# Loading the first keys uncast on SyncE's queue, in a fused pooled-attention and mixture-of-experts kernel

## The chip, the cores and the metric

The kernel runs on one core of one Trainium2 chip. The metric is the device time of one execution in microseconds (us); the kernel before was quoted at 178.73 us, the median of 6 runs (178.28 to 179.21).

Five engines work on such a core: TensorE (PE in the profile, PEld for its weight loads), VectorE (DVE), ScalarE (ACT), GpSimd (POOL) and SyncE (SP). Data is moved by 16 DMA engines. GpSimd feeds them through the *software queue*, which in this kernel casts float32 to bfloat16 on the way (a row of 18,432 B read is written as 9,216 B); what SyncE and ScalarE send through their queues here is not cast.

## The reference, cut to what matters

```python
# q, k, v: (8 batches, 8 heads, 576, 64) float32
k_p = k.reshape(B, H, 72, 8, D).mean(axis=3)          # keys pooled by 8
v_p = v.reshape(B, H, 72, 8, D).mean(axis=3)
attn = softmax(q @ k_p.T / sqrt(D)) @ v_p
x = attn, rearranged to (4608, 512)
logits = x @ phi                                       # phi: (512, 32)
slot_input = softmax(logits, axis=0).T @ x             # 32 slots, 4 for each of 8 experts
slot_out[e] = relu(slot_input[e] @ w1[e]) @ w2[e]      # w1: 512x1024, w2: 1024x512, float32
out = softmax(logits, axis=1) @ slot_out               # (4608, 512) float32
```

The inputs are 62 MB of float32 and the output is 9.4 MB. The kernel computes in bfloat16.

## The kernel before: the parts that matter here

The batches are worked on in four pairs. For each pair, k, q and v are loaded whole (one tile is 128 partitions by 72 rows of 64 values), cast by the software queue. All these tiles share four buffers, so a load waits until PE has finished with the tile four loads earlier. The weights w1 and w2 follow in the same queue.

```python
big = ctx.enter_context(tc.tile_pool(name="big", bufs=4))

def load_pair(src, pair, name):
    t = big.tile([128, NT, D], BF, name=name, tag="big")
    nc.gpsimd.dma_start(out=t, in_=src[2 * pair:2 * pair + 2].rearrange("b h (i t) d -> (b h i) t d", t=NT))
    return t

w1_sb = persist.tile([128, E, DJ, F], BF)
...
phi_f = persist.tile([128, DM // 128, NS], FP)
nc.sync.dma_start(out=phi_f, in_=moe_phi.rearrange("(p j) e -> p j e", j=DM // 128))   # 64 KB
k_sb[0] = load_pair(k, 0, "k_sb")
q_sb[0] = load_pair(q, 0, "q_sb")
... # identity matrix, made by GpSimd
v_sb[0] = load_pair(v, 0, "v_sb")
...
for pair in range(1, NP):          # k, q, v of the other pairs, then w1, then w2
    ...
```

PE pools k (`pool_ps`), transposes q (`q_ps`), pools v, and so on; `place_phi` spreads phi into a constant on VectorE (`spread`) for a later matmul.

The softmax here doesn't subtract the row's maximum and nothing guards it: scores larger than these inputs give would overflow.

Of the kernel before, what the change touches and what calls it, by code (L numbers as in the profile page):

```python
# [8 lines left out]
FP = mybir.dt.float32  # L9
BF = mybir.dt.bfloat16  # L10
# [8 lines left out]
def kernel(  # L19
# [10 lines left out]
    nc = tc.nc  # L30

    B, H, S, D = q.shape
# [3 lines left out]
    E = moe_w1.shape[0]  # L36
# [8 lines left out]
    NT = S // NI  # L45
# [13 lines left out]
    big = ctx.enter_context(tc.tile_pool(name="big", bufs=4))  # L59
# [7 lines left out]
# [6 lines that stand above are left out]
# [23 lines left out]

    k_sb, q_sb, v_sb = [None] * NP, [None] * NP, [None] * NP

    phi_f = persist.tile([128, DM // 128, NS], FP)
    nc.sync.dma_start(out=phi_f, in_=moe_phi.rearrange("(p j) e -> p j e", j=DM // 128))  # L100

    hT = persist.tile([128, E, FJ, NS], BF)
    k_sb[0] = load_pair(k, 0, "k_sb")
    q_sb[0] = load_pair(q, 0, "q_sb")
    ident = consts.tile([128, 128], BF)
    make_identity(nc, ident)
# [31 lines left out]
    for r in range(2):  # L138
        rows = slice(r * D, (r + 1) * D)
        nc.vector.tensor_copy(out=iphi[rows, :, 0:D],  # L140
                              in_=ident[rows, rows].rearrange("p d -> p () d").to_broadcast([D, H, D]))
# [7 lines left out]
    so = persist.tile([128, DM], BF)  # L149
    recC = persist.tile([128, 1], FP)  # L150
    recR = persist.tile([128, NSMALL + (NO - NSMALL) // 2, 4], FP)

    for pair in range(1, NP):
        for dst, src, name in ((k_sb, k, "k_sb"), (q_sb, q, "q_sb"), (v_sb, v, "v_sb")):
# [244 lines left out]
    for n in range(E // NG):  # L399
        for half in range(F // 512):  # L400
            cols = slice(half * 512, (half + 1) * 512)
            h_ps = ps_m.tile([128, 512], FP, name="h_ps", tag="m")
            for j in range(DJ):
                for g in range(NG):
                    e = n * NG + g
# [112 lines left out]
```

## Time and profile before

| what | before |
|---|---|
| span of the profiled run | 175.8 us (175.764) |
| DMA engines, 2.5 to 140 us | share 0.97 to 1.08 in windows of 2.5 us, about 214 GB/s written |
| effective start of the weight-and-input stream, mean engine | 3.72 us |
| last weights landed, mean engine / slowest engine | 148.78 / 149.58 us |
| first and last output packet | 149.52 / 173.62 us |

First the profile's 40 equal slices of the span for the kernel before: a digit is the busy share of the slice in tenths, and the last row is what the DMA engines moved. Below them are its queue totals: packets, megabytes written, and packet time as a share of 16 engines.

```profile
PE   7992899699999999999999898799975295787000
...
DMA  4999999999999999999999999999999999999994
GB/s 72 206 222 210 222 214 210 224 212 220 210 223 212 218 216 210 223 211 216 214 214 216 214 214 218 214 214 218 213 218 214 208 193 167 334 362 425 420 418 190
...
q0 software_dynamic: 6816, 30.94, 86.8%
q1 hardware_dynamic: 3872, 9.50, 13.9%
```

The DMA engines are full from the second slice to the last but one. The software queue writes bfloat16 at about 214 GB/s, which means that it reads float32 at about 428 GB/s; the output at the end is plain float32 at about 420 GB/s. So this is a kernel bound by its DMA engines: its time is when they start, plus their work, plus any holes.

Next the same kernel in windows of time. The columns are: window and its length, busy time (and count) of PE, PEld, DVE, ACT and POOL, PE's granted clock, the share of the DMA engines, and GB/s. A window's share may exceed 1 because a packet is counted where it begins.

```profile
0.00:2.00 2.00, 0.81 (x2) 0.28 (x3) 1.10 (x11) 1.26 (x1) 0.95 (x6) 1.00 0.08 24
2.00:3.00 1.00, 1.00 (x4) 0.43 (x3) 0.20 (x1) 0.23 (x2) 0.93 (x3) 1.00 1.34 147
3.00:4.00 1.00, 1.00 (x4) 0.33 (x3) 0.88 (x5) 0.00 (x0) 1.00 (x3) 1.00 0.04 9
4.00:5.00 1.00, 1.00 (x3) 0.30 (x2) 1.00 (x7) 0.00 (x0) 0.11 (x1) 1.00 1.14 230
...
20.00:40.00 20.00, 17.39 (x188) 12.04 (x186) 8.02 (x22) 13.28 (x26) 1.59 (x3) 0.84 1.03 215
```

Until 2.6 us only the 64 KB of phi have been moved. The large packets counted from 2 to 3 us are the first fourteen of the software queue; they are slow and occupy their engines until about 4 us, and from then on the engines run at full rate. That poor stretch is what the change is after; I call it empty below.

The trace also has one record per DMA packet, with queue, start, duration and size. Each load ends on each of the 16 engines with a 4-byte completion packet. In this text *landing on the mean engine* is the mean of those 16 times and *on the slowest engine* the last of them. The sizes that matter in the records of the kernel before:

| packet | median duration |
|---|---|
| software queue, one row of k, q or v (9,216 B written, 18,432 B read) | 0.700 us (one begins every 0.684 us) |
| software queue, one row of w1 (8,192 B written) | 0.625 us |
| SyncE's queue, 8,192 B of output | 0.314 us |
| software queue, 512 B piece of the last w2 | 0.060 us |

### The profile page before, as it was taken

The numbers are of one execution on the slowest core, as the hardware profiler recorded it, in microseconds if no ns is written. First come the engines' busy times: TensorE is split into PE (matmuls) and PEld (weight loads), VectorE is DVE, ScalarE is ACT, GpSimd is POOL, SyncE is SP. The second block draws the span as 40 slices with busy tenths as digits, with TensorE's granted clock in tenths as the row PEclk, the third lists the DMA queues.
The fourth block names the chain that finished last, engine by engine and source line by source line (L and its number), as shares of the span: only waits on it lengthen the run. The fifth ranks groups of instructions, "written<-read, shape, count | busy, mean of one in ns | idle before, by whom it ended". The sixth has DMA issues, their size and how long they took to land.

```text
span 175.8 us, 3531 instructions
## 1 busy us (share of the span) xinstructions
PE 140.2 (80%) x1469; PEld 88.2 (50%) x1469; DVE 90.9 (52%) x252; ACT 80.3 (46%) x146; POOL 19.7 (11%) x39
## 2 busy tenths in 40 slices
PE   7992899699999999999999898799975295787000
PEld 2452677464987667876676435563564132321000
DVE  5401612456387796877978718953351005799000
ACT  3021289456395696946979724011110003699000
POOL 6001110002011071111113002101400000000000
PEclk9999699855599999999999758559999569999655
DMA  4999999999999999999999999999999999999994
GB/s 72 206 222 210 222 214 210 224 212 220 210 223 212 218 216 210 223 211 216 214 214 216 214 214 218 214 214 218 213 218 214 208 193 167 334 362 425 420 418 190
DMA packets 10702, 40.64 MB, mean 231 GB/s; under 512 B 832, under 2 KB 6336, under 8 KB 6592
## 3 DMA queue, kind: packets, MB, share of 16 engines
q0 software_dynamic: 6816, 30.94, 86.8%
q1 hardware_dynamic: 3872, 9.50, 13.9%
q8 instruction: 11, 0.18, 0.4%
q14 instruction: 3, 0.02, 0.0%
HBM read 61.93 MB, written 9.44 MB: 406 GB/s over the span
## 4 chain that ended last, share of the span: by engine, by line
PE 45%; DMA 30%; ACT 10%; DVE 3%; issue 2%; POOL 1%; POOLq 0%; ACTq 0%
DMA w_xs<-in_moe_w_dram 14%; DMA q_sb<-in_q_dram 11%; PE pool_ps L181 8%; PE sc L250 8%; PE u_ps L262 8%; PE G_ps L279 6%; DMA k_sb<-in_k_dram 5%; PE q_ps L195 5%; PE f_ps L464 3%; ACT w_sb L466 2%; DVE xs L268 2%; PE lg_ps L273 2%; PE fold_ps L206 2%; ACT ex_1634 L251 1%; ACT ex_1635 L251 1%
## 5 line engine op out<-in xcount | busy, mean ns | idle before, releaser
L268 DVE TENSOR_TENSOR xs<-u_ps,rec 128x384 bf16<-128x384 f32 x72 | 39.4, 551 | 1.6
L250 PE MATMUL sc<-qT,kp 64*72 64x288 bf16 x128 | 24.4, 327 | 0.8 <-ACT ex_1635 L251 0.4
L267 DVE RECIPROCAL rec<-u_ps 128x4 f32<-128x4 f32 x72 | 12.4, 175 | 20.2 <-PE u_ps L262 19.9
L195 PE MATMUL q_ps<-ident,q_sb 128*128 128x128 bf16 x144 | 13.7, 250 | 5.3 <-DMA q_sb<-in_q_dram 5.0
L201 DVE COPY qT<-q_ps 128x768 bf16<-128x768 bf16 x16 | 8.8, 551 | 16.7 <-PE q_ps L195 16.6
L195 PEld LDWEIGHTS <-q_sb 128*128 128x128 bf16 x144 | 10.4, 113 | 7.3 <-DMA q_sb<-in_q_dram 5.3
L464 PE MATMUL f_ps<-so,cT 128*128 128x512 bf16 (+1 forms) x46 | 11.0, 331 | 3.6 <-DVE so L453 1.2
L250 PEld LDWEIGHTS <-kp 64*72 64x72 bf16 x128 | 8.9, 111 | 8.8 <-issue 3.5
L279 PE MATMUL G_ps<-xs,ee 128*128 128x512 bf16 x36 | 11.8, 471 | 0.4 <-ACT ee L274 0.4
L181 PE MATMUL pool_ps<-pmat,v_sb 128*128 128x128 bf16 x144 | 11.2, 240 | 0.0
L199 ACT COPY qT<-q_ps 128x768 bf16<-128x768 bf16 x8 | 6.4, 799 | 9.8 <-PE q_ps L195 9.7
L114 PEld LDWEIGHTS <-zeros 128*128 128x128 bf16 x51 | 5.7, 120 | 9.6 <-issue 5.9
L184 ACT CAST kpar<-pool_ps 128x512 bf16<-128x512 f32 (+1 forms) x12 | 5.5, 485 | 10.7 <-PE pool_ps L181 10.6
L181 PEld LDWEIGHTS <-v_sb 128*128 128x128 bf16 x144 | 9.7, 109 | 0.8 <-issue 0.3
L181 PE MATMUL pool_ps<-pmat,k_sb 128*128 128x128 bf16 x144 | 9.7, 219 | 0.2
L466 ACT ACTIVATE o_sb_2313<-f_ps,recR 128x256 f32<-128x256 f32 x1 | 0.5, 474 | 19.7 <-PE f_ps L464 19.7
L464 PEld LDWEIGHTS <-cT 128*128 128x128 bf16 x46 | 4.3, 96 | 10.0 <-issue 7.6
L181 PEld LDWEIGHTS <-k_sb 128*128 128x128 bf16 x144 | 8.4, 98 | 1.2 <-DMA k_sb<-in_k_dram 0.6
L468 DVE TENSOR_SCALAR w_sb<-f_ps,recR 128x512 f32<-128x512 f32 x12 | 8.3, 746 | 0.0
L184 ACT CAST vpar<-pool_ps 128x512 bf16<-128x512 f32 (+1 forms) x12 | 5.6, 480 | 5.8 <-PE pool_ps L181 5.7
L453 DVE TENSOR_SCALAR so<-so_ps_2183,recC 128x256 bf16<-128x256 f32 x1 | 0.5, 484 | 14.5 <-PE so_ps_2183 L449 14.5
L466 ACT ACTIVATE w_sb<-f_ps,recR 128x512 f32<-128x512 f32 x12 | 7.7, 684 | 0.6
(165 smaller groups left out, 240.2 us busy)
## 6 DMA issues: line engine op xcount, KB each, us to landing
w_sb<-in_moe_w_dram POOLq DMA_DIRECT2D x7, 1024.0 KB, 28.3
out_dram<-w_sb SPq DMA_DIRECT2D x6, 1024.0 KB, 8.5
k_sb<-in_k_dram POOLq DMA_DIRECT2D x4, 1152.0 KB, 17.8
q_sb<-in_q_dram POOLq DMA_DIRECT2D x4, 1152.0 KB, 17.9
v_sb<-in_v_dram POOLq DMA_DIRECT2D x4, 1152.0 KB, 16.2
w_big<-in_moe_w_dram POOLq DMA_DIRECT2D x4, 1024.0 KB, 30.4
w_qT<-in_moe_w_dram POOLq DMA_DIRECT2D x2, 1024.0 KB, 34.8
w_xs<-in_moe_w_dram POOLq DMA_DIRECT2D x2, 512.0 KB, 24.2
```

The source lines that it names most:

```text
L181: nc.tensor.matmul(out=ps[:, r].rearrange("p n i -> p (n i)"), lhsT=src[:, tt:tt + 2, :].rearrange("p t d -> p (t d)"), rhs=pmat, start=(t ...
L184: nc.scalar.copy(out=dst[:, r0:r0 + nr], in_=ps[:, 0:nr])
L195: nc.tensor.transpose(out=ps[:, t].rearrange("p n i -> p (n i)"), in_=q_sb[pair][:, tt:tt + 2, :].rearrange("p t d -> p (t d)"), identity= ...
L201: nc.vector.tensor_copy(out=dst, in_=ps)
L250: nc.tensor.matmul(out=ps[:, r, 0:S // 2], lhsT=kp[pair][rows, n], rhs=qT[pair][rows, n], start=True, stop=True)
L262: nc.tensor.matmul(out=ps[rows, hh], lhsT=ex[b][:, hh].rearrange("p r t -> p (r t)")[:, c:c + rows.stop - rows.start], rhs=vp[(2 * pair + ...
L267: nc.vector.reciprocal(out=rec, in_=ps[:, :, XW])
L268: nc.vector.tensor_tensor(out=xs[pair][:, t, qd * HQ:(qd + 1) * HQ, :], in0=ps[:, :, 0:XW], in1=rec.rearrange("p h -> p h ()").to_broadcas ...
L279: nc.tensor.matmul(out=ps, lhsT=ee[:, t].rearrange("p g s -> p (g s)"), rhs=x[:, t, :, 0:D], start=(t == 0), stop=(t == 8))
L464: nc.tensor.matmul(out=f_ps, lhsT=rows(r), rhs=so[:, cols], start=True, stop=True)
L466: nc.scalar.activation(out=o_sb[:, r], in_=f_ps, func=AF.Copy, scale=recR[:, g, r:r + 1])
L468: nc.vector.tensor_scalar(out=o_sb[:, r], in0=f_ps, scalar1=recR[:, g, r:r + 1], scalar2=None, op0=ALU.mult)
```

## The change

The intent is to start earlier. SyncE's queue can begin before the software queue does, so the first k is sent there, uncast, into space that the last three experts' w1 will need only much later. VectorE and ScalarE then cast it. The software queue begins with q.

```diff
+    k_f = w1_sb[:, E - 3:E].rearrange("p e j f -> p (e j f)").bitcast(FP)[:, 0:NT * D].rearrange("p (t d) -> p t d", d=D)
+    k_rows = k[0:2].rearrange("b h (i t) d -> (b h i) t d", t=NT)
+    k_cuts = ((0, 32), (32, NT))
+    for t0, t1 in k_cuts:
+        nc.sync.dma_start(out=k_f[:, t0:t1], in_=k_rows[:, t0:t1])
     phi_f = persist.tile([128, DM // 128, NS], FP)
     nc.sync.dma_start(out=phi_f, in_=moe_phi.rearrange("(p j) e -> p j e", j=DM // 128))
 ...
-    k_sb[0] = load_pair(k, 0, "k_sb")
+    k_sb[0] = big.tile([128, NT, D], BF, name="k_sb", tag="big")
     q_sb[0] = load_pair(q, 0, "q_sb")
 ...
+    for t0, t1 in k_cuts:
+        th = (t0 + t1) // 2
+        nc.vector.tensor_copy(out=k_sb[0][:, t0:th], in_=k_f[:, t0:th])
+        nc.scalar.copy(out=k_sb[0][:, th:t1], in_=k_f[:, th:t1])
```

## The prediction

> **What bounds the kernel now.** The 16 DMA engines. In the 40 slices DMA reads 9 from the second to the last slice but one; in the windows its share is 0.97 to 1.06 from 2.5 us to 140 us at about 214 GB/s written (429 GB/s read, as the software queue casts float32 to bfloat16), and in the output phase 410 to 423 GB/s. PE is 80% busy; in the chain of waits the last weights take 24.7 us from issue to landing: backlog, not a late issue. So the time is the engines' start, plus their work, plus holes.
>
> **What the change does.**
> - Engine work stays. The Trainium skill, "DMA: Bandwidth & Descriptors", section "Issuing engines are not separate DMA queues", says both queues run on the same 16 engines. In the packet records a cast packet (9,216 B written, 18,432 B read) takes 0.70 us (steps of 0.684); a plain 8,192 B packet on SyncE's queue takes 0.314 us (outputs). The same row in float32, 8 KB plus 10 KB, is an estimated 0.69 to 0.71 us. Eight rows per engine: 5.5 to 5.65 us against 5.47 us.
> - The start moves. SyncE's phi, issued at 0.74 us, has its first packets at 1.74 us. The software queue's first packets start at 2.64 us and take 1.07 to 1.87 us instead of 0.70; the first k load ends at 8.79 us on its fastest engine and 10.35 us on its slowest, so the effective start is 3.3 to 4.9 us. With k on SyncE's queue the engines work from about 1.75 us and the slow software start hides under it: 1.5 us gained on a fast engine, up to 3 us on the slowest. I take 2.
> - Added: four casts, by estimate 1 to 1.4 us each, on DVE and ACT, idle there. phi lands behind k; harmless.
> - k itself should land later: q shares the engines. If they alternate packet by packet (same page, "Queues, rings and completion order"), 0.31 us of k go against 0.70 us of q, about a third for k. Estimate: first cut at 7 to 8 us, second at about 16 us (before: all at 10.4), q at about 12 us (before 15.8). PE's k pooling then ends near 19 us (before 12.9), q transposes near 23 us (before 20.4).
>
> **On the critical path.** The PE slip is not: PE waits at 30.4 to 32.5 us for the second q, which absorbs most of it, and software loads are issued 6 to 12 us before the queue runs dry (second q at 13.2 us against 25.2, third v at 40.1 against 47.1). These margins shrink to about 2 to 5 us; I expect no hole. So the 2 us of earlier start should arrive at the end almost whole.
>
> **Predicted:** 176.8 us, range 175.5 to 178.4. Faster by over 2% (under 175.2): 0.08; within 2%: 0.90; slower by over 2%: 0.02.
>
> **What would show it.** Packets of SyncE's queue near 1.75 us with DMA share near 1 from then; first q's packets from about 2.6 us, k's second cut after 13 us; DMA share without holes at 20 to 70 us; last weight landing near 147.6 us (before 149.6); output phase as long as before (about 24 us).
>
> **What would make it wrong.** Packets of the two queues together running slower or faster than alone; k squeezed so far that the second q is issued too late (after 22 us) and the queue runs dry; the slow engine late for a reason that the start doesn't cure (then only 0 to 1 us); a changed clock history of PE.

## More of the kernel before

At the end the last w2 comes in column halves, so that the first output rows can leave while the second half is still landing:

```python
nc.gpsimd.dma_start(out=w2_sb[E - 2][:, 0:j], in_=src[E - 2][:, 0:j])        # j = 5 of 8
for c in range(2):
    cols = slice(c * DM // 2, (c + 1) * DM // 2)
    nc.gpsimd.dma_start(out=w2_sb[E - 2][:, j:FJ, cols], in_=src[E - 2][:, j:FJ, cols])
    nc.gpsimd.dma_start(out=w2_sb[E - 1][:, :, cols], in_=src[E - 1][:, :, cols])
```

## The result, and the profile after

The changed kernel takes 177.53 us, the median of 10 runs (176.8 to 178.42), against 178.41 us for the kernel before (20 runs, 177.44 to 179.21). The ratio is 0.9963, with a 95% interval of 0.9937 to 0.9989. Ratios here are the mean time of one kernel's fast runs over that of the other's of the same rounds, so they are not quite the ratio of the medians quoted. In microseconds it is 0.0037 x 178.4 = 0.66 us faster. The prediction was 1.93 us; the measured time lies within its range, but the gain is a third of what was said.

The lines of the changed kernel that answer to those above, first the slices and queues:

```profile
PE   7965389999999999999999896898862295787000
...
DMA  5999999999999999999999999999999999999995
GB/s 191 321 290 216 213 218 212 217 220 215 210 215 216 219 215 217 213 215 219 213 215 213 221 213 215 215 213 222 213 213 215 208 193 155 317 364 422 419 423 211
...
q0 software_dynamic: 6672, 29.76, 83.4%
q1 hardware_dynamic: 4160, 11.86, 17.6%
```

The work has moved from one queue to the other: the shares of the two add up to 100.7% before and to 101.0% after. The higher GB/s at the start is only that uncast bytes are counted on the written side.

The windows of the changed kernel:

```profile
0.00:2.00 2.00, 0.81 (x2) 0.28 (x3) 1.10 (x11) 1.26 (x1) 0.95 (x6) 1.00 0.35 53
2.00:3.00 1.00, 1.00 (x4) 0.43 (x3) 0.19 (x1) 0.22 (x2) 0.93 (x3) 1.00 0.52 172
3.00:4.00 1.00, 1.00 (x4) 0.33 (x3) 0.00 (x0) 0.00 (x0) 0.56 (x2) 1.00 0.95 393
4.00:5.00 1.00, 1.00 (x3) 0.30 (x2) 0.00 (x0) 0.00 (x0) 0.00 (x0) 1.00 1.04 428
...
20.00:40.00 20.00, 17.24 (x180) 12.98 (x180) 8.50 (x22) 11.12 (x22) 1.58 (x3) 0.72 1.03 216
```

The engines come near full rate (393 GB/s uncast, then 428) at 3 us rather than at 4, not at 1.75 us. Between 2 and 3 us they move 172 GB/s. And there is no hole later: 1.03 from 20 to 40 us, as before.

The DMA issues of the changed kernel (what, by whose queue, how often, size, us from issue to landing):

```profile
w_sb<-in_k_dram SPq DMA_DIRECT2D x1, 1280.0 KB, 12.9
w_sb<-in_k_dram SPq DMA_DIRECT2D x1, 1024.0 KB, 4.9
phi_f<-in_moe_phi_dram SPq DMA_DIRECT2D x1, 64.0 KB, 18.3
```

And two of the longest waits of its first 40 us (who waited, for whom, us in total, how often, longest):

```profile
POOL q_sb L69 <- ACT kpar L194: 14.3, 1, 14.3
...
DVE spread L235 <- DMA phi_f<-in_moe_phi_dram: 4.2, 1, 4.2
```

phi needs 18.3 us (1.8 us before): it stands behind k's second cut until about 13 us, and then its small packets take turns with large ones of the software queue, from 12.9 to 18.9 us. VectorE stands 4.2 us at `spread` for it, with the copies of q behind it. PE's transposes of the first q end at 24.9 us; before they ended at 20.2 us. So the attention part begins almost 5 us late, although the kernel is faster.

From the packet records, the landings on the mean engine, and what is left of the gain at each:

| point | before | after | gain |
|---|---|---|---|
| effective start (first cut, or first k, less its work at full rate) | 3.72 | 2.57 | 1.15 |
| first q | 14.66 | 13.69 | 0.97 |
| first v | 20.13 | 19.41 | 0.72 |
| second k | 25.66 | 24.88 | 0.78 |
| second v | 36.67 | 35.89 | 0.78 |
| last weights, mean engine | 148.78 | 148.09 | 0.69 |
| last weights, slowest engine | 149.58 | 149.30 | 0.28 |

(Effective start: before, 9.19 us landing less 8 x 0.684 = 5.47; after, 5.04 us landing of the first cut less 8 x 0.309 = 2.47.) The gain on the mean engine is made in the first microseconds, shrinks to 0.7 us by 20 us, and then stays to the end. It agrees with the timed 0.66 us. The slowest engine's last landing is from one profile each and scatters more. Yet it is the one that sets the time of a single run: in 12 of the 13 profiled runs of this document the time of the run itself is 27.9 to 28.3 us after that landing, and the first output packet begins within 0.06 us of it (the exception, `e9_whole_w2`, comes last below). Less 28.1 us, the mean times of all runs, 178.26 and 177.59 us, put the slowest engine at about 150.2 and 149.5 us: an estimate, and 1.4 us behind the mean engine in both kernels. So on average it gains what the mean engine gains, and the 0.28 us of this pair of profiles is partly chance.

### The profile page after: what moved, and what is told of

Read it like the earlier page. It is cut to its first block, busy times and chain, and to the rows that moved or that the text cites. A ratio compares the mean times of both kernels' runs of the same rounds, so it can differ in the third digit from the quotient of the medians.

```text
span 175.3 us, 3538 instructions
## 1 busy us (share of the span) xinstructions
PE 136.8 (78%) x1469; PEld 87.3 (50%) x1469; DVE 92.0 (52%) x254; ACT 81.9 (47%) x148; POOL 19.0 (11%) x38
## 4 chain that ended last, share of the span: by engine, by line
PE 47%; DMA 26%; ACT 13%; DVE 5%; issue 1%; SPq 0%; DVEq 0%; ACTq 0%
DMA w_xs<-in_moe_w_dram 15%; DMA phi_f<-in_moe_phi_dram 10%; PE pool_ps L191 9%; PE sc L260 8%; PE u_ps L272 7%; PE q_ps L205 5%; PE G_ps L289 5%; PE f_ps L474 3%; ACT w_sb L476 2%; DVE xs L278 2%; PE fold_ps L216 2%; PE lg_ps L283 2%; ACT ex_1639 L261 1%; ACT ex_1640 L261 1%; PE lg_ps_1918 L283 1%
## 5 line engine op out<-in xcount | busy, mean ns | idle before, releaser
L260 PE MATMUL sc<-qT,kp 64*72 64x288 bf16 x128 | 22.9, 308 | 0.8 <-ACT ex_1640 L261 0.4
L205 PE MATMUL q_ps<-ident,q_sb 128*128 128x128 bf16 x144 | 13.1, 241 | 3.2 <-DVE qT L211 2.8
L191 PE MATMUL pool_ps<-pmat,k_sb 128*128 128x128 bf16 x144 | 10.9, 232 | 3.5 <-DVE k_sb L160 3.4
L191 PEld LDWEIGHTS <-k_sb 128*128 128x128 bf16 x144 | 9.4, 104 | 4.4 <-DVE k_sb L160 3.5
L289 PE MATMUL G_ps<-xs,ee 128*128 128x512 bf16 x36 | 9.8, 407 | 0.4 <-ACT ee L284 0.4
L459 PEld LDWEIGHTS <-hT 128*32 128x32 bf16 x128 | 3.6, 105 | 10.4 <-issue 10.2
## 6 DMA issues: line engine op xcount, KB each, us to landing
v_sb<-in_v_dram POOLq DMA_DIRECT2D x4, 1152.0 KB, 12.9
w_sb<-in_k_dram SPq DMA_DIRECT2D x1, 1280.0 KB, 12.9
```

Of the source, the lines that this page charges most:

```text
L191: nc.tensor.matmul(out=ps[:, r].rearrange("p n i -> p (n i)"), lhsT=src[:, tt:tt + 2, :].rearrange("p t d -> p (t d)"), rhs=pmat, start=(t ...
L205: nc.tensor.transpose(out=ps[:, t].rearrange("p n i -> p (n i)"), in_=q_sb[pair][:, tt:tt + 2, :].rearrange("p t d -> p (t d)"), identity= ...
L260: nc.tensor.matmul(out=ps[:, r, 0:S // 2], lhsT=kp[pair][rows, n], rhs=qT[pair][rows, n], start=True, stop=True)
L289: nc.tensor.matmul(out=ps, lhsT=ee[:, t].rearrange("p g s -> p (g s)"), rhs=x[:, t, :, 0:D], start=(t == 0), stop=(t == 8))
```

## The experiments

Two theories were set against each other.

- **S**: every engine-microsecond counts, before and after, and PE's lateness costs nothing. Then the loss is at the start itself: the empty time that could be filled was simply smaller than 2 us.
- **R**: the start gave about 2 us as predicted, and 1.3 us of it was lost later, through VectorE's wait for phi and PE's late begin.

Three side questions came up: when the software queue begins (theories P, T and Q in the texts on record), what phi costs, and whether engine time saved at the end of the stream counts as well. All runs gave correct results. The table has them all; the columns of packet records are one profile each, in us.

| run | ratio to before (95%) | mean start of the first 16 large packets | second k, mean engine | last weights, mean / slowest |
|---|---|---|---|---|
| before | 1 | 2.90 | 25.66 | 148.78 / 149.58 |
| changed | 0.9963 (0.9937 to 0.9989) | 1.93 | 24.88 | 148.09 / 149.30 |
| e4_before_extra | 1.0127 (1.0094 to 1.0161) | 2.41 | 27.75 | 151.22 / 153.10 |
| e11_extra_first | 1.0090 (1.0061 to 1.0119) | 1.90 | 27.28 | 150.38 / 151.49 |
| e3_after_extra | 1.0115 (1.0079 to 1.0151) | 1.91 | 27.44 | 150.53 / 151.46 |
| e2_phi_scalar | 0.9969 (0.9935 to 1.0004) | 2.00 | 24.83 | 147.93 / 149.04 |
| e1_phi_first | 0.9976 (0.9945 to 1.0006) | 2.46 | 25.20 | 148.29 / 150.41 |
| e6_first_cut | 0.9965 (0.9928 to 1.0002) | 1.93 | 24.78 | 148.05 / 150.04 |
| e7_first_cut_phi_scalar | 0.9969 (0.9934 to 1.0004) | 1.97 | 24.82 | 148.15 / 149.09 |
| e12_half_cut | 0.9973 (0.9944 to 1.0002) | 1.92 | 25.13 | 148.22 / 149.44 |
| e5_before_small | 1.0045 (1.0008 to 1.0082) | 2.38 | 25.78 | 149.18 / 151.11 |
| e8_short_first | one look, 178.16 us | 1.85 | 25.00 | 148.13 / 149.88 |
| e9_whole_w2 | 1.0012 (0.9983 to 1.0041) | (not used) | 24.75 | 147.76 / 148.67 |

### How much empty time there was: a useless load, in three places

The first adds to the kernel before a load that nobody uses, behind phi:

```diff
     nc.sync.dma_start(out=phi_f, ...)
+    spare_f = w1_sb[:, 1:3] ... .bitcast(FP)[:, 0:32 * D] ...
+    nc.sync.dma_start(out=spare_f, in_=k[2:4].rearrange("b h (i t) d -> (b h i) t d", t=NT)[:, 0:32])
```

> The kernel before, plus a useless float32 load of 8 KB per partition (1 MB) on SyncE's queue behind phi, so that SyncE's queue has work at the start as in the changed kernel, but nothing is taken from the software queue. The load costs each engine 8 packets of 0.309 us = 2.47 us. Theory S (the usable empty time at the start is small, about 1.15 us per engine, since the first packets of either queue are slow): 2.47 - 1.15 = about 1.3 us slower than before (0.9 to 1.6), ratio 1.007. Rival R (the start gave the 2 us that were predicted and 1.3 us of it were lost later, through the PE slip): the empty time takes 2 us, so about 0.5 us slower (0.2 to 0.7), ratio 1.003.

Measured: ratio 1.0127, which is 0.0127 x 178 = 2.3 us slower; both theories had said less (1.3 and 0.5). The first k landed at 11.27 us on the mean engine, 2.08 us later than before, so of the load's 2.47 us only 0.4 us fell into empty time. The records say why S was off: behind phi the load's packets began at 2.41 us on average, half a microsecond later than k's do in the changed kernel, and its first 16 packets took 0.94 us each instead of 0.31. I had left out phi's place in the queue. A rival with more empty time is further off still.

The second run puts the same two lines into the changed kernel, behind phi:

> The changed kernel plus the same useless load of 1 MB, behind phi on SyncE's queue. No empty time is left there. S: engine time counts in full, 2.47 us more than the changed kernel, so about 1.8 us slower than before (1.4 to 2.2), ratio 1.010. If the time after the start had slack, as R needs where PE sets the end of the stream, the extra load would cost clearly less than 2.47 us. The difference between this and the other extra load, set against the kernel before, is by S only what the change itself gives (about 0.5 us).

Measured: 1.0115, 2.0 us slower than before, so about 2.7 us slower than the changed kernel (0.0115 + 0.0037 = 0.0152, x 178). At the second k the records show 27.44 against 24.88: 2.56 us, the load's own 2.47 us and little else. Engine time in the stream counts in full; there is no slack in it. (The two runs with the load behind phi differ by 0.2 us, 1.0127 less 1.0115, where the text on record had about 0.5; the intervals allow either.)

The third repeats the first with the two lines ahead of phi:

> The kernel before with the useless 1 MB load again, but issued ahead of phi, so that it begins at about 1.74 us as k does in the changed kernel (behind phi it began at 2.24 us, its first packets were slow, and it cost 2.08 us at the software queue's first landing). Theory S, sharpened: the load's 2.47 us of engine time run from an effective 2.6 us (mean start 1.93 plus 0.6 of slow first packets) to about 5.0; the first k then lands on the mean engine at about 10.5 to 10.8 us (before 9.19, behind phi 11.27), the whole is 1.3 to 1.7 us slower than before, ratio 1.008, about 0.5 us less than with the load behind phi. Against S: if the place in SyncE's queue does not matter, 1.0127 again.

Measured: 1.0090, 1.6 us slower than before; first k at 10.81 us on the mean engine. Both are as S says when phi is no longer in front, the landing at the upper end. So the empty time that such a load can use is 2.47 - (10.81 - 9.19) = 0.85 us with phi behind it, about 1.1 us if phi's own time (below) is counted back, and not 2. This is R's first half refuted by a kernel in which PE, VectorE and ScalarE do nothing new.

### Whether PE's lateness cost anything

```diff
-    nc.sync.dma_start(out=phi_f, in_=moe_phi.rearrange("(p j) e -> p j e", j=DM // 128))
+    nc.scalar.dma_start(out=phi_f, in_=moe_phi.rearrange("(p j) e -> p j e", j=DM // 128))
```

> The changed kernel with phi issued by ScalarE's queue at the start instead of behind k on SyncE's. phi lands before 4 us instead of 19.6 us; the copies of q on VectorE no longer stand behind readers of phi; the PE slip shrinks by about 3 us. S: only phi's share of engine time in the middle of the stream comes back, 0.1 to 0.3 us against the changed kernel, so 0.8 to 1.0 us faster than before, ratio 0.995. R: the slip was what cost the rest, so 1.5 to 2 us faster than before, ratio 0.990.

Measured: 0.9969, as the changed kernel; R's 0.990 lies outside the interval. The issues of the software queue on GpSimd show how far PE moved: they wait until PE has freed a buffer. Columns: start, duration, instruction, and in brackets the wait ahead of it and what ended it. First the third and fourth v and the fourth k of the changed kernel, then the same of this one:

```profile
43.06 0.53 POOL L69 DMA_DIRECT2D v_sb<-in_v_dram  x1 [4.91 <-PE sc L260]
48.35 0.53 POOL L69 DMA_DIRECT2D k_sb<-in_k_dram  x1 [4.24 <-PE u_ps L272]
...
61.70 0.53 POOL L69 DMA_DIRECT2D v_sb<-in_v_dram  x1 [7.46 <-PE sc L260]
```

```profile
38.21 0.53 POOL L69 DMA_DIRECT2D v_sb<-in_v_dram  x1 [4.92 <-PE sc L260]
43.50 0.53 POOL L69 DMA_DIRECT2D k_sb<-in_k_dram  x1 [4.24 <-PE u_ps L272]
...
56.85 0.53 POOL L69 DMA_DIRECT2D v_sb<-in_v_dram  x1 [7.46 <-PE sc L260]
```

PE runs 4.9 us earlier, the loads are issued 4.9 us earlier, and the time is the same. They only wait longer in the queue. R falls. The chain of waits of the changed kernel would have misled here; these are two of its pieces (start, length, what):

```profile
1.64 18.29 DMA phi_f<-in_moe_phi_dram
...
119.24 26.72 DMA w_xs<-in_moe_w_dram
```

The chain gives phi 10.4% of the span, since at each step it follows whatever released the instruction last. But the last w2 waited 26.72 us in a full queue, so everything ahead of its issue had slack, phi included.

This run also prices phi. In the changed kernel first v lands 19.41 - 13.69 = 5.72 us after first q on the mean engine; here it is 19.30 - 13.83 = 5.47 us, the plain work of eight rows. phi in the middle of the stream takes 0.25 us from every engine. Here phi went among the first packets of k instead (2.2 to 5.6 us, landed for VectorE at 6.0, not before 4 as expected), and the first q landed 0.14 us later.

The counter-test puts phi in front on the same queue, which frees PE as well but delays k:

```diff
+    phi_f = ...; nc.sync.dma_start(out=phi_f, ...)
     for t0, t1 in k_cuts:
         nc.sync.dma_start(out=k_f[:, t0:t1], in_=k_rows[:, t0:t1])
-    phi_f = ...; nc.sync.dma_start(out=phi_f, ...)
```

> The changed kernel with phi issued first on SyncE's queue and k behind it. In the first extra-load run the load behind phi had its first packets at 2.24 us against 1.74 us for k in the changed kernel. Theory S (the gain is only the earlier beginning of large packets, engine time counts in full): k begins 0.5 us later (0.4 to 0.9 with slower first packets), phi's 0.25 us in the middle of the stream comes back: 0.2 to 0.5 us worse than the changed kernel, so 0.1 to 0.5 us faster than before, ratio 0.998. Rival R (waiting behind phi on VectorE and the PE slip cost the rest of the predicted gain): phi lands at 2.3 us, so faster than before by 1.3 us or more, ratio 0.993 or less.

Measured: 0.9976, what S said (0.998). The large packets begin at 2.46 us instead of 1.93, and at the second k 0.32 us of the gain is gone (25.20 against 24.88), which is the 0.53 us of later start less about 0.25 us of phi. R's 0.993 or less lies outside the interval.

### The smallest load that fills the start

```diff
-    k_cuts = ((0, 32), (32, NT))
+    k_cuts = ((0, 32),)
     k_sb[0] = big.tile([128, NT, D], BF, name="k_sb", tag="big")
+    nc.gpsimd.dma_start(out=k_sb[0][:, 32:NT], in_=k_rows[:, 32:NT])
```

> Only the first cut of k (8 KB of 18 KB per partition) comes in float32 by SyncE's queue; the second cut is cast by the software queue, at its head, before q. The start is covered as in the changed kernel, k is complete at about 8.5 to 9.5 us (13.9 in the changed kernel, 10.4 before), and PE is ahead of the kernel before. S: about as the changed kernel or slightly better, 0.6 to 1.0 us faster than before, ratio 0.995 to 0.997. R: with the PE slip gone the whole predicted gain appears, 1.5 to 2 us faster, ratio 0.990.

> First cut of k alone in float32 by SyncE's queue, second cut cast at the head of the software queue, phi by ScalarE's queue: both single changes that did no harm, together. S: engine time is the changed kernel's less about 0.3 us (phi under the start, less float32 at 0.70 instead of 0.684 us a row): 0.8 to 1.1 us faster than before, ratio 0.994 to 0.996. R would have 0.990.

Measured: 0.9965 and 0.9969 (the second also has phi on ScalarE's queue). k is complete at 8.3 us on the mean engine in both, earlier than in either original, and the time is that of the changed kernel. The 0.3 us that I hoped for in the second did not show: at the second k it stands at 24.82 against 24.88. R's 0.990 is excluded by both.

With half of that cut, 4 KB per partition:

> As the run with the first cut alone and phi by ScalarE's queue, but the cut is 16 rows (4 KB per partition, eight packets of about 0.155 us per engine) instead of 32. SyncE's queue then has work until about 3.8 us only. Theory T (the software queue's first packets come at 5.0 to 5.4 us whenever SyncE's queue has a large load in flight at the start, however it is cut): the engines stand empty from about 3.8 to 5.1 us, and the kernel is as the one before or slower by up to 0.8 us, ratio 1.000 to 1.004. Theory Q (the software queue starts when SyncE's queue lets it): it starts at 3.5 to 4 us and the gain stays, ratio 0.996 to 0.997.

Measured: 0.9973. The software queue's first packets began at 3.63 to 4.18 us, so theory Q holds and T, as stated, falls. The gain at the second k is 0.53 us.

### When the software queue begins

I had predicted its first packets from 2.6 us, alternating with k's. They began at 5.16 us, although GpSimd issued the load at 1.25 us in both kernels. Two runs ask why.

```diff
-    k_cuts = ((0, 32), (32, NT))
+    k_cuts = ((0, 8), (8, NT))
```

> The changed kernel with k cut at 8 of 72 rows instead of 32: eight packets of 2 KB and then eight of 16 KB per engine. It asks why the software queue's first packets came at 5.16 us and not at 2.6 us as predicted. Theory P (SyncE's queue had about 9 packets per engine fetched ahead, which are served before the first change of queue): the first 9 packets now take about 1.8 us instead of 3.3, so the software queue starts at 3.5 to 4.5 us. Rival T (the software queue was not ready before about 5.1 us, whatever SyncE's queue holds): it starts at 5.1 to 5.4 us again. Time: as the changed kernel within 0.5 us by S.

Measured: 5.32 us, against P (3.5 to 4.5) and at T's number. But the run above, with 3.63 us, had refused T. One more, a small useless load in the kernel before (`[:, 0:8]` in place of `[:, 0:32]` in the first diff):

> The kernel before with a useless load of 2 KB per partition (0.26 MB, eight packets of about 0.084 us per engine, 0.67 us in all) behind phi on SyncE's queue. Theory T: the software queue, which started at 2.63 us with phi alone ahead of it, starts after 5 us; first k on the mean engine at 10.3 us or later, 1.0 to 1.5 us slower than before, ratio 1.007. Theory Q: it starts at 3.0 to 3.6 us and the cost is at most the load's own, 0.2 to 0.7 us, ratio 1.001 to 1.004.

Measured: 3.12 to 3.92 us for the first packets, as Q says, and T falls again. The time is 1.0045, 0.8 us slower, more than the 0.12 us at the second k and 0.40 us at the last weights on the mean engine explain; the interval reaches down to 1.0008. What the records show: with a large load in front, the software queue did not cut in until SyncE's first load was worked off or nearly so. The earliest completion of that load on an engine is at 4.61 us in the changed kernel (software from 5.16), 4.63 us with the extra load first (4.82), 3.60 us with the half cut (3.63), 3.12 us with the small load (3.12), and 5.60 us with the extra load behind phi (5.41). With the short first cut it completed at 2.69 us but the software queue began at 5.32 us, some packets of 16 KB later. How many packets, or bytes, of a second load go ahead was not settled. Nor is a mixture of the theories excluded: in all ten profiled runs with 8 KB or more per partition on SyncE's queue the software queue began at 4.82 to 5.41 us, so that it may be ready at about 5 us while SyncE's queue has work, and sooner only where that queue runs empty. The cause of the late start stays open.

### Engine time taken away at the end

```diff
-        nc.gpsimd.dma_start(out=w2_sb[E - 2][:, 0:j], in_=src[E - 2][:, 0:j])
+        nc.gpsimd.dma_start(out=w2_sb[E - 2], in_=src[E - 2])
         for c in range(2):
             cols = slice(c * DM // 2, (c + 1) * DM // 2)
-            nc.gpsimd.dma_start(out=w2_sb[E - 2][:, j:FJ, cols], in_=src[E - 2][:, j:FJ, cols])
             nc.gpsimd.dma_start(out=w2_sb[E - 1][:, :, cols], in_=src[E - 1][:, :, cols])
```

> The changed kernel with engine time taken away elsewhere: the second last w2 comes as whole rows (one 8 KB packet of 0.625 us per row) instead of one of 5 KB (0.399 us) and six of 512 B (0.060 us each), 0.76 us. Eight rows per engine: 1.1 us of engine time less, at the very end of the weight stream. S: time falls by 0.7 to 1.2 us against the changed kernel (a little may come back where output now starts later behind the weights), so 1.4 to 1.9 us faster than before, ratio 0.990. If the end of the stream were set by something other than the engines' work, nothing would change: ratio 0.996.

Measured: 1.0012, so the gain of the changed kernel is gone: a miss for S as I stated it. First, the engine time taken away was far less than 1.1 us: the 512 B packets overlap, and one begins on an engine every 0.042 us although each takes 0.060 (the DMA share from 144 to 146 us is 1.46). With the steps of the records, 0.383 us for 5 KB and 0.609 for 8 KB, eight rows save an estimated 0.2 us. The last weights did land 0.33 us earlier on the mean engine and 0.63 us on the slowest. Second, the first column half of the last w2, which the first output needs, now stands behind all of the second last w2 and landed at 146.02 us on the slowest engine instead of 145.64. The first output packet left at 149.67 us instead of 149.28. Windows at the end, first of the changed kernel and then of this one, columns as above:

```profile
148.00:150.00 2.00, 1.82 (x22) 0.80 (x21) 1.70 (x4) 1.75 (x5) 0.00 (x0) 1.00 0.60 154
150.00:152.00 2.00, 1.08 (x10) 0.66 (x8) 1.55 (x4) 0.95 (x3) 0.00 (x0) 1.00 1.02 344
152.00:154.00 2.00, 1.76 (x8) 0.70 (x8) 1.92 (x5) 1.79 (x4) 0.00 (x0) 1.00 1.00 341
```

```profile
148.00:150.00 2.00, 1.61 (x11) 0.64 (x13) 1.88 (x5) 1.77 (x5) 0.00 (x0) 0.74 0.29 70
150.00:152.00 2.00, 1.40 (x19) 0.72 (x12) 0.79 (x3) 0.41 (x1) 0.00 (x0) 0.50 1.01 344
152.00:154.00 2.00, 1.96 (x9) 0.90 (x8) 1.79 (x4) 1.68 (x4) 0.00 (x0) 0.50 0.83 289
```

From 148 to 150 us the engines stood at a share of 0.29 with nothing to move, where the changed kernel without this edit had 0.60. The 0.39 us by which the output begins late is the landing's: from PE's first matmul on that column half (146.40 us here, 146.01 without the edit) to the issue of the first output it is 2.02 us in both. Another 0.33 us went in the output phase (24.44 us against 24.11), in which the share from 152 to 154 us is 0.83 instead of 1.00. There PE's granted clock was 0.50 instead of 1.00, and its matmuls ahead of the half rows took 353 ns on average instead of 271; that this made the second hole is likely, but was not tried. The two together are the 0.72 us between the profiled runs (178.08 and 177.36 us). Engine time counts where something is waiting to use it. In the changed kernel the tail is balanced: the output's start and the last landing fall within 0.02 us of each other (149.28 and 149.30).

No version beat the changed kernel by more than the intervals.

## Why the prediction was right or wrong, point by point

**Right: what bounds the kernel.** The prediction rested on the Trainium skill, "DMA: Bandwidth & Descriptors", section "Issuing engines are not separate DMA queues", that both queues run on the same 16 engines. The trace agrees: sending k uncast saved no engine time (100.7% and 101.0% of packet time), and a useless load of 2.47 us on the other queue made the changed kernel 2.6 us later at the second k.

**Right: PE's lateness is harmless, and no hole appears.** DMA share 1.03 from 20 to 80 us in both kernels; PE almost 5 us earlier gave nothing (e2_phi_scalar). The third v was issued at 43.06 us, and the load ahead of it ended on the fastest engine at 46.47 us: a margin of 3.4 us, within the 2 to 5 us predicted.

**Right: the size of the uncast row.** 8 KB in 0.309 us and 10 KB in 0.398 us are 0.707 us a row, inside the estimated 0.69 to 0.71, and eight of them cost 0.2 us more than cast rows do.

**Right in part: where k lands.** First cut predicted at 7 to 8 us, landed at 5.04 us; second cut at about 16 us, landed at 13.33 us on the mean engine (13.85 on the slowest); q at about 12 us, landed at 13.69. The page's section "Queues, rings and completion order" says that an engine goes round the queues packet by packet. The trace agrees from about 5.8 to 12 us, where each engine sends a 0.398 us packet of k and a 0.699 us packet of q in turn every 1.07 us, but shows no turns before that: k's first cut had the engines to itself, and the software queue came at 5.16 us and not at 2.6 us. (A packet of the page holds several descriptors; I had taken each packet record for one, and no run shows how the two relate.)

**The step that failed: "The start moves ... 1.5 us gained on a fast engine, up to 3 us on the slowest. I take 2."** The mechanism was right, and this term of the sum was too large:

- I took the effective start of the new stream to be its first packet, 1.75 us, but that of the old stream to be its first packet plus its slow start. The slow start is not the software queue's own. In the kernel before, the first 16 packets took 1.37 us instead of 0.70, and slow packets cost 0.72 us per engine in all; in the changed kernel SyncE's first 16 took 0.81 us instead of 0.309, and slow packets cost 0.61 us per engine. Only the beginning moved, from a mean of 2.90 to 1.93 us, 0.97 us. The effective start went from 3.72 to 2.57: 1.15 us, not 2.
- From that go 0.18 us by the first q (uncast rows and alternation) and 0.25 us by the first v: phi, which I had called harmless. The wait that it caused on VectorE and PE was harmless to the time (e2_phi_scalar), but before it ran in empty time for nothing and now it runs in a full stream. That leaves 0.72 us, and 0.69 us at the end on the mean engine.
- The extra for the slowest engine did not last. At the second k the slowest engine landed 1.54 us earlier, at the last weights 0.28 us. The trace shows eleven 16 KB packets of an instruction queue in each kernel, of about 0.95 us, spread over the run. In the kernel before, at each of the ten that fall into the software queue's stream of large packets, one engine's stream stands still for 0.87 to 0.98 us, from the start of the instruction packet to its end within 0.03 us (followed by chaining packets in time, since the records name no engine). So each such packet takes its own time from one engine, and eleven of them cannot fall evenly on sixteen engines: which engine is last at the end can thus be decided on the way. That this eats the slowest engine's gain is argued from those records; no run took the instruction packets away. The prediction had named such a case ("the slow engine late for a reason that the start doesn't cure"), but did not reckon with it.

**Right in the letter, wrong in what it was taken for: "DMA share near 1 from" 1.75 us.** The packets begun by 3 us took 2 x 0.35 + 0.52 = 1.22 us per engine, which fills the time since 1.75 us; but the first of them are the slow ones, and the engines moved 172 GB/s from 2 to 3 us against 393 from 3 us. A busy engine is not yet one at full rate. **Wrong: the last weights near 147.6 us.** They landed at 149.30 us. **Right: the output phase** took 24.1 us from first to last packet in both kernels.

## What to carry to other kernels

Where a stream is full from its first microseconds to its end, as here, starting it earlier paid once, by as much as its first *large* packets were moved forward (0.97 us), less what the change added to the stream; the slow first packets were paid by whichever queue went first, so compare like with like when estimating an empty start. A small transfer that ran for nothing in an empty stretch costs engine time once that stretch is filled, and a wait that the chain of waits shows is worth nothing as long as the transfers it delays would have queued anyway. A useless load of known size, put into the supposed gap, measures the gap directly, if it stands where the real load would: behind phi it began half a microsecond late.

## What the Trainium skill lacked or had wrong

- "DMA: Bandwidth & Descriptors", specifications: first byte after about 1 us on the software path and 0.6 us on the other. Here SyncE's first packets began 1.00 us after issue (0.74 to 1.74 us) and the software queue's 1.38 us (1.25 to 2.63 us); the difference agrees (0.38 us). Both absolute figures are larger when counted from the start of the issuing instruction; from its end they are 0.62 us (from 1.12) and 0.69 us (from 1.94). The page does not say which it counts from.
- No page gives it that the first large packets of an execution are slow on either queue: 0.81 us instead of 0.309 (8 KB, SyncE's), 1.37 us instead of 0.70 (software); 0.4 to 0.9 us per engine in all over the runs. Small packets ahead (phi) did not take it away (0.94 us instead of 0.309 in `e4_before_extra`).
- The same page, "Queues, rings and completion order", has queues taking turns by packets, of typically 9 to 17 descriptors. At the start the software queue got no turn before 5.16 us in the changed kernel and 3.63 us with half the cut, with the same issue at 1.25 us. Eight rows and a completion on each engine may be one such packet, so this does not show the page wrong, though with a short first cut, done at 2.69 us, the turn came no sooner (5.32 us). What the page lacks is for how long one queue can hold off another at the start.
- No page gives the cost of instruction loading to a full DMA stream ("Runtime: NRT & Kernel Launch", section "Instruction fetch mechanics", tells of refills in blocks of 16 KiB, but not what other transfers lose): eleven packets of 16 KB, about 0.95 us each, each holding up one engine.
